# A new hand-written order table for a fused attention and feed-forward kernel, and one rule for its warm-up products

## The chip, the cores and the metric

The kernel runs on one core of a Trainium2 chip. The metric is device microseconds of one launch. Five engines work side by side: TensorE (PE; its weight loads are listed as PEld), VectorE (DVE), ScalarE (ACT), GpSimd (POOL) and SyncE (SP), which here only issues transfers. Each engine takes its instructions strictly in the order of its own list and waits at the head of that list, so an order of the lists is an order of the work.

## The reference: what is computed

The input x is one sequence of 2048 rows of 640 numbers. It is normalised by rows; the normalised rows feed two branches whose results are added to x.

```
xn  = layernorm(x)                              # 2048 x 640
q   = xn @ wq -> 32 heads of 20;  k = xn @ wk, v = xn @ wv   # one shared head of 20
p   = softmax(q k^T * 20**-0.5);  o = p v       # 32 heads x 2048 x 2048
A   = concat(o) @ wo
B   = relu(xn @ w1 + b1)**2 @ w2 + b2           # 640 -> 1536 -> 640
out = x + A + B
```

Almost all of the work outside TensorE is the exponential of 32 x 2048 x 2048 scores.

## The kernel before, in words

**Tiles.** A block is four heads by 512 query rows; there are 32 blocks, and each has 16 tiles of 128 keys. For one key tile the four heads make four score products of 128 x 512 into four banks of PSUM, called QK when ScalarE takes the exponential and DQK when VectorE does. Seven banks go round among the scores and the other products; the eighth collects the weighted sums of a block.

**Two ways to an exponential.** ScalarE takes two banks in one instruction (line 1328, names ACT0 to ACT695), 696 in all, and the product PV with v follows. The other way is a "set" (164 sets, one key tile of one block each): VectorE makes an integer approximation of the scores from each bank (line 1551, D1_n_i), three shifted copies of that table of 128 x 2048 are made by passes P1, P2 and P3, each either on GpSimd (line 1571, two joined ones line 2117) or on VectorE (line 1572), and the four terms are multiplied with v (DPV). Two of the four terms of a set (a = 0 and a = 3) can be added into another table instead of being multiplied: either by a transfer that GpSimd issues and that adds on landing (lines 1588, 2047, 2115; AD), or by VectorE (lines 1593, 2048). So of every set there are five choices.

**The opening.** The first rows of x come in four transfers of 128 rows (X0 to X3) and later ones in larger pieces (X4, X6, X8, and X12 for rows 1536 to 2047, line 753). Per 128 rows: statistics (lines 806 to 808, S and AG; VE is line 803 or 811), the power -1/2 on GpSimd (line 820, PW), the normalised rows (line 822, XN, on VectorE or GpSimd), a transpose on TensorE (lines 866 and 934, T) and its copy out of PSUM (lines 869, 871 and 937, TE). From these come kT (KTe, lines 885 and 949), the first queries (Q0 products, and their copies Qe0 on ScalarE, line 887) and v. A copy xb of x in device memory is made by SP (line 1152), and a transfer XA that GpSimd issues (line 1153) adds the bias b2 onto it; xb plus b2 is the residual that is added to the outputs much later (XR loads). SP waits for the copy TE2 before it issues wq (line 764) or xb. Before the first transposes TensorE makes products of constants (line 905, "warm-up products"), and later products of zeros onto the summing bank ("zero products", kT with zeros on line 729); in the planner's list both have the name fill, the second kind with the mark tail.

**The other work.** The feed-forward products FFN (960 products), their relu and square on VectorE (RL line 1054, SQ line 1062), the output products OUT and the last ones OF (line 729 for all of TensorE), the normalisation of blocks (TN line 1416, R on line 1422, CM on line 1452, with small transfers between) run between the scores.

**What sets the order.** A planner in the kernel first builds each engine's list by priorities. Then the table PLAN reorders it: for PE, DVE, POOL and SP each number says which of the instructions still left is next (0 is the first left, and n*k stands for n taken k times); "held" says for each POOL operation which VectorE operation it has to wait for, since some operations of the two (marked lock) are kept apart; and "on" has one digit for each choice: five digits a set, three for the passes (0 GpSimd, 1 VectorE) and two for the terms a = 0 and a = 3 (0 multiplied, 1 added by a transfer, 2 added by VectorE). ScalarE's list has no table and keeps its order. A function replay then walks through the reordered lists with a table of durations and gives out the PSUM banks and buffers; the waits follow from that. Behind replay a loop drops zero products that would fall where no block's sum is open.

## Time and profile before

| | |
|---|---|
| time, median of 3 runs | 665.14 us (664.26 to 666.17) |
| the profiled execution | 664.67 us |
| its span | 662.9 us |
| busy, ACT / PE / DVE / POOL | 649.2 / 655.0 / 627.0 / 533.1 us |
| first and last exponential on ScalarE | start at 12.17, end at 653.85 us |

The span runs from the first instruction to the last one in the profile; some 1.8 us of the execution lie around it. A row of a group reads: line, engine, operation, out<-in, shapes, count, then busy time and the mean of one in ns, then the idle time before them with what ended it. A row of the timeline has the start in us, the length in us, and the count of instructions merged into it. The starts of two neighbouring exponentials lie closer together than one lasts, so a stretch of n of them lasts n-1 spacings and one duration.

### The profile page before, as it was taken

What the parts mean: (1) busy time and instruction counts of PE and PEld (TensorE: products, weight loads), DVE (VectorE), ACT (ScalarE), POOL (GpSimd) and SP (SyncE); (2) the same over time, 40 slices, a digit from 0 to 9 for tenths busy, and PEclk for the clock granted to TensorE, in tenths of its full rate; (3) what the DMA queues carried; (4) which work ended last, traced back from release to release, by engine and by line L of the source; (5) the groups of instructions that cost most, each with busy time, mean ns of one, the idle gap of its engine ahead of it and who ended that gap; (6) DMA issues with size and microseconds to landing.
All of it is one profiled execution on the core that took longest, in us unless ns stands there. A gap on an engine that the chain in (4) does not pass through costs nothing. (4 is left out here: it accounts for less than half of the span.)

```text
span 662.9 us, 22377 instructions
## 1 busy us (share of the span) xinstructions
PE 655.0 (99%) x9569; PEld 212.6 (32%) x9570; DVE 627.0 (95%) x1125; ACT 649.2 (98%) x719; POOL 533.1 (80%) x528
## 2 busy tenths in 40 slices
PE   8999999999999999999999999999999999999997
PEld 4432222332322223333332222333233322223444
DVE  8979999999999999999999999999999999999997
ACT  7999999999999999999999999999999999999995
POOL 1629899898998889898999988888899989799300
PEclk9999999999999999999999999999999999999999
DMA  8694967788997995786956645798798655858731
GB/s 262 188 238 113 189 126 161 163 183 190 191 192 162 184 182 114 135 177 124 184 103 152 126 92 102 153 180 176 150 176 167 130 123 98 171 104 183 136 113 68
DMA packets 53528, 102.09 MB, mean 154 GB/s; under 512 B 15916, under 2 KB 31164, under 8 KB 53364
## 3 DMA queue, kind: packets, MB, share of 16 engines
q0 software_dynamic: 18544, 68.17, 55.7%
q1 hardware_dynamic: 34308, 32.11, 16.7%
q8 instruction: 75, 1.23, 0.8%
q10 hardware_dynamic: 576, 0.38, 0.2%
q14 instruction: 25, 0.20, 0.1%
HBM read 23.26 MB, written 10.01 MB: 50 GB/s over the span
## 5 line engine op out<-in xcount | busy, mean ns | idle before, releaser
L1328 ACT ACTIVATE PT<-ps 128x1024 bf16<-128x1024 f32 x696 | 640.1, 1125 | 1.8 <-PE ps L729 1.4
L1551 DVE TENSOR_SCALAR tx<-ps 128x512 uint16<-128x512 f32 x656 | 423.7, 682 | 20.8 <-PE ps L729 13.5
L1571 POOL INT64_ADD tx<-tx x369 | 391.2, 1130 | 56.7 <-PE ps L729 16.4
L729 PE MATMUL ps<-qT,kT 20*128 20x512 bf16 x2048 | 263.5, 385 | 0.3
L729 PEld LDWEIGHTS ps<-qT,kT 20*128 20x128 bf16 x2048 | 67.8, 91 | 253.1 <-ACT PT L1328 133.5
L729 PE MATMUL ps<-PT,vx 128*32 128x512 bf16 x1392 | 131.4, 384 | 0.0
L729 PE MATMUL ps<-tx,vxs 128*32 128x512 bf16 x1220 | 113.0, 384 | 0.6 <-DMA tx<-tx 0.5
L1588 POOL DMA_DIRECT2D tx<-tx x103 | 102.4, 994 | 7.7 <-POOL tx L1571 6.9
L729 PE MATMUL ps<-w_sb,big 128*32 128x320 bf16 x1536 | 82.7, 302 | 0.0
L729 PE MATMUL ps<-tx,vx 128*32 128x512 bf16 x864 | 81.3, 384 | 0.8 <-DMA tx<-tx 0.7
L729 PE MATMUL ps<-xnT,w_sb 128*32 128x512 bf16 x960 | 79.0, 383 | 0.0
L1572 DVE TENSOR_SCALAR tx<-tx 128x2048 uint16<-128x2048 uint16 x91 | 63.0, 705 | 0.5 <-DMA tx<-tx 0.3
L729 PEld LDWEIGHTS ps<-PT,vx 128*32 128x32 bf16 x1392 | 34.4, 95 | 39.5 <-issue 35.0
L729 PEld LDWEIGHTS ps<-w_sb,big 128*32 128x32 bf16 x1536 | 34.2, 96 | 30.9 <-issue 20.7
L729 PEld LDWEIGHTS ps<-tx,vxs 128*32 128x32 bf16 x1220 | 28.7, 95 | 36.6 <-issue 27.7
L1054 DVE TENSOR_SCALAR hT_tmp<-ps,b1col 128x512 bf16<-128x512 f32 x48 | 35.7, 743 | 1.5 <-PE ps L729 1.3
L729 PE MATMUL ps<-xnT,wq_sb 128*32 128x512 bf16 (+2 forms) x480 | 35.6, 356 | 0.0
L729 PE MATMUL ps<-wo_c,OC 128*32 128x320 bf16 x576 | 31.8, 301 | 0.0
L2117 POOL INT64_ADD tx<-tx x16 | 30.6, 1913 | 0.5
L729 PEld LDWEIGHTS ps<-tx,vx 128*32 128x32 bf16 x864 | 21.0, 95 | 27.1 <-issue 20.5
L729 PEld LDWEIGHTS ps<-xnT,w_sb 128*32 128x32 bf16 x960 | 19.4, 95 | 25.7 <-issue 17.4
L1416 DVE COPY OR<-ps 128x512 f32<-128x512 f32 x30 | 20.4, 681 | 0.9 <-PE ps L729 0.6
(91 smaller groups left out, 242.3 us busy)
## 6 DMA issues: line engine op xcount, KB each, us to landing
tx<-tx POOLq DMA_DIRECT2D x111, 512.0 KB, 5.8
tx<-tx POOLq DMA_DIRECT2D x7, 1024.0 KB, 9.3
w_sb<-in_B_w_dram SPq DMA_DIRECT2D x8, 480.0 KB, 9.3
big<-OR SPq DMA_DIRECT2D x71, 40.0 KB
xb<-in_A_x_dram SPq DMA_DIRECT2D x1, 2560.0 KB, 12.7
xb<-b2r POOLq DMA_DIRECT2D x1, 2560.0 KB, 19.1
xr<-xb SPq DMA_DIRECT2D x16, 160.0 KB, 3.5
out_dram<-out_sb SPq DMA_DIRECT2D x15, 160.0 KB, 3.3
```

What stands on the lines that cost most here:

```text
L729: return lambda e: e.matmul(out_(), l, val(r), start=val(start), stop=val(stop), tile_position=tp, skip_group_check=loose)
L1054: o = Op(f"RL{qc}_{f}", "DVE", 0.66, [lambda e: e.tensor_scalar(out=hT_tmp[:, k % 2, :], in0=ps[:, at(bk), :], scalar1=b1col[:, f:f + 1], ...
L1328: o = Op(f"ACT{st_['j']}", "ACT", ACB + ACM * n, [lambda e: e.activation(out=PT[:, slots[0].n:slots[0].n + n, :], in_=src(), func=AF.Exp, ...
L1416: tn = op(f"TN{b}", "DVE", 0.60, lambda e: e.tensor_copy(out=OR[:, a, :], in_=ps[:, PVB, :]), [lastpv] + or_users[a], prio=0)
L1551: d1 = op(f"D1_{n}_{i}", "DVE", 0.60, lambda e: e.tensor_scalar(out=L()[:, cs].bitcast(U16), in0=ps[:, ref.n, :], scalar1=XA, scalar2=XB, ...
L1571: fns = dict(POOL=lambda e, T=T, j=j: e.int64_add(out=T().bitcast(I64), in0=L().bitcast(I64), in1=TSTEP * j * 0x0001000100010001), DVE=lam ...
L1572: DVE=lambda e, T=T, j=j: e.tensor_scalar(out=T().bitcast(U16), in0=L().bitcast(U16), scalar1=TSTEP * j, scalar2=None, op0=ALU.add))
L1588: p = op(f"AD{a}_{n}", "POOL", ADDUR, lambda e, src=src, dst=dst: e.dma_start(dst(), src(), accum_op=ALU.add), dp + [ad_last.get(k)], dma= ...
L2117: fn = lambda e, x=x: e.int64_add(out=two(*sorted((x["ref"][2].n, x["ref"][3].n))).bitcast(I64), in0=two(*sorted((x["ref"][0].n, x["ref"][ ...
```

## The change

Every list of PLAN is new. Most entries of the choices stay: 54 of the 820 digits of "on" differ. Counted over the sets, passes on GpSimd go from 401 to 395 and on VectorE from 91 to 97; terms that are multiplied go from 193 to 191, those added by a transfer from 125 to 127, and those added by VectorE stay 10.

Read against the planner's lists, which are the same in both kernels, the new order table says this, among much else:

- SP: `X8, X12, b2, wq, xb, w11, b1, w10` becomes `X8, b2, xb, X12, wq, b1, w10`; some weights (w11, w12, w13, w20 to w23) come later among the small transfers.
- PE: `K0, Q0_0, Q0_1, Q0_3, K1, Q0_2, K2, V0_0, V0_1, K3, QK0, QK1` becomes `K0, Q0_1, Q0_0, Q0_3, Q0_2, K1, V0_1, K2, QK1, QK0`, with K3 behind.
- Warm-up products: ahead of the first transpose 15 become 12, between it and the first weighted sum 3 become 5, and one stands behind that sum. Of the zero products 12 stay in the kernel before and 8 in the new one.
- POOL: `PW13, PW12, XA, PW14` becomes `PW12, XA, PW13, PW14`; the XA issue comes behind the statistics of tile 12 in both.
- DVE: ahead of XN12 and XN13 there were `AG12, VE13, S14a, VE12, S15b, KTe5, Ve2`; between VE12 and XN12 there are now `TE10, TE11, S13b, S14a, S14b, AG13, KTe5, VE13, S15b, Ve2`.
- DVE, up to set 144: ten passes more than before; behind it fewer, so that six more remain.
- PE changes between score products and other products 1322 times instead of 1318. Behind the last score product QK695 there were 9 OUT, 40 OF, 3 PV and 1 DPV; now there are 8, 40, 3 and 3.

The second part is in the loop behind replay: a warm-up product that would come after the first weighted sum has begun is left out.

```diff
     "PE": (
-        "0*39 1 2 16 21 4 0 28 1*2 2 0 15 1*2 2*3 4 2 21 2*3 30 4 3 2 30 0 1 0 7 0 5 4 0*4 1 0*3 49 0*2 1*7 0*2 1 2 1 0 7 1*7 0*3 1*3 3 2*2 1 0 1*7 2 3 2 0 2 3 2 0*2 1*11 2 5 2*2 "
...
+        "0*8 55 39 0 68 0*2 2 4 0 42 3*6 4 3*2 4 3 5 3 6 5 17 6 3 29 3 0 2 4 55 3 9 3*2 5*2 27 44 5*2 2 5*3 7 5*2 0 4 3 1 5 4 12 3 1 2 0 6*2 1*10 2 0 8 0 1*3 0*4 1*2 36 1 8 2*7 1 "
...
     "DVE": (
...
     "POOL": (
-        "0*15 2 0*7 1 0 2 5 0*2 4 0 5 3 5 6*2 5 7 9 5 2 0 5 12 3 7 5 3 0 4 0*2 1 4 1 4 0 1 0 4 0 4 1*2 0*2 3 0 1 2 3 0*2 4 2 4 0*2 1 2 0*2 1 0 1 0 2 0*2 1 3*2 0*2 2 0 2*5 1 2 3 "
...
+        "0*2 1 0*22 2 1*2 5 3 6 7 4 7 0 7 2 4 6 8 5 14 0 3*2 0*3 3 8 2 3 1 2 1 0 1 0 1 4 0*3 2 5 0*3 1 2 3 0 3 6 2 1 0 2 0 1 0*2 4 1 0*2 2*2 0 4 0 1 0 3 0 3*2 4 3*2 6 0 1 4 0 1 6 "
...
     "SP": (
-        "0*10 2 1 0 5 2 0*2 2*3 4 1*2 2 5*3 12 2 10 18 9 1*2 19 2 10 17 6 0 15 7 5 2 16 11 4 10 20 8 4 0 14 7 13 3 20 3 7 6 12 9 5 16 19 4 9*2 3 5 20 11 0 10 11 8 10 8 10 4 14 12 "
...
+        "0*6 1 2 0*2 1 0 7 5 6*2 8 12 6 11 7 1 0 8 5 14*2 13 0 2*2 1 8 1 7 18 4 17*2 8*2 15*2 17 2 11 5*2 18*2 12 10 5 1 13 12*2 5 4 20 0 5 8 10 4 12 14 12 0 14*2 11 8 7 16 9 3 2 "
...
     "held": (
-        "-*2 31*2 51 - 57 51 57 30 - 57 30 - 51 - 51 - 102 - 102 103 -*2 132 126 -*6 146*2 149 -*2 174*2 149 -*17 174 216 186 - 224*2 - 224 - 224 - 241 224 -*6 252 241 -*2 252 260 "
...
+        "-*2 29 30 50 51 57*2 51 57*2 - 57*2 50 -*6 106 -*3 130 141 - 147*5 121 - 141 -*7 179*2 -*7 192 - 173 192 - 212 - 212 - 212 223 212 -*4 242 -*2 241 242 - 252 242 -*3 252 "
...
     "on": (
-        "01000000000000100000100110000000010000100000001001000100001000000000000000001010000100000000110011100001000010000200001000010001100001010000001100011000010010100011010010"
-        "00010000100011100000100100001001010000100010001010000100011000010010110101000010000110001000010100100001000100000000001001010001100000001010000011101000111000000001000110"
-        "01111000200000000010110000001000011000011101001000000100010100002000010100100000000000001000110000000001000000000100011000000000000000000010000100100000011000000000000010"
-        "10010001100101000110100100001001011000000001001010110111001000000100100101000010000101010000010000101001001010001100101000000010100111000000000100001000010010100000000010"
-        "00000010100000000000000100001001010000101000001010100100001100000000000001010010000000001001000100100011001011001101110211122111201112211120"),
+        "01000000000000100000010110000000010000100000001001000100011000000000000010001010000100000000010110100001000010001200001000010001101001000000001100011000010010100011010110"
+        "00010000100011100000100100001001010000100010000010100100011000010010110001010010001110001000010100100001000100001001001001010001100000001010000011101000111000000001000110"
+        "00111000200000000010100000001000011000011011001000000100010100002000010100110000001000001000011000001001000000000100011000000001000000000010000101000000011000000000000010"
+        "00010010100001000110100100001001011000000001001010100111001001000010100001000010001101010000010000101101011010010100011000000010100111000000000100001000010010100000000010"
+        "10001000100000000000000100011001010000100010000010100100001100000000000001010010000000001001000100100011000011001101110211122111201112211120"),
@@ -2145,11 +2149,12 @@
             es_.sort(key=lambda o: o.start)
             for o in es_:
                 o.ends[0], o.ends[1] = o is es_[0], o is es_[-1]
-        open_, kept = set(), []
+        open_, kept, begun = set(), [], False
         for o in order_all:
             if o.sums is not None:
                 (open_.discard if o.ends[1] else open_.add)(0)
-            if o.name == "fill" and o.tail and not open_:
+                begun = True
+            if o.name == "fill" and (not open_ if o.tail else begun):
                 continue
             kept.append(o)
         order_all[:] = kept
```

## The prediction

> **What bounds the kernel now.** I read the share of each engine first, then the row of the exponentials, then the timeline of ScalarE alone.

> ```profile
> PE 655.0 (99%) x9569; PEld 212.6 (32%) x9570; DVE 627.0 (95%) x1125; ACT 649.2 (98%) x719; POOL 533.1 (80%) x528
> ...
> L1328 ACT ACTIVATE PT<-ps 128x1024 bf16<-128x1024 f32 x696 | 640.1, 1125 | 1.8 <-PE ps L729 1.4
> ```

> ```profile
> 12.17 152.22 ACT L1328 ACTIVATE PT<-ps 128x1024 bf16<-128x1024 f32 x165 [0.23 <-PE ps L729]
> 164.71 127.69 ACT L1328 ACTIVATE PT<-ps 128x1024 bf16<-128x1024 f32 x139 [0.32 <-PE ps L729]
> 292.65 170.95 ACT L1328 ACTIVATE PT<-ps 128x1024 bf16<-128x1024 f32 x186 [0.25 <-PE ps L729]
> ...
> 556.13 97.72 ACT L1328 ACTIVATE PT<-ps 128x1024 bf16<-128x1024 f32 x106 [0.19 <-PE ps L729]
> ...
> 657.06 1.63 ACT L1662 ACTIVATE out_sb<-ps 128x320 bf16<-128x320 f32 x4 [3.21 <-PE ps L729]
> ```

> ScalarE makes one exponential after the other from 12.17 to 653.85 us (556.13 + 97.72), with 1.8 us of idle time before all 696. So the execution is a head of 12.2 us, 641.7 us of exponentials, and a tail of 9.0 us, in which ScalarE waits 3.21 us for TensorE. The change touches neither the number nor the shape of the exponentials. Only three things can move the time: the head, the spacing of the exponentials, and the tail. The spacing is (164.71 - 12.17) / 165 = 0.9245 us in the first stretch, (292.65 - 164.71) / 139 = 0.9204 us in the second. A short stretch shows what it is when little is late:

> ```profile
> 560.88 11.11 ACT L1328 ACTIVATE PT<-ps 128x1024 bf16<-128x1024 f32 x12
> ```

> Here it is (11.11 - 1.125) / 11 = 0.908 us. All 695 spacings at that value would give 695 x (0.9219 - 0.908) = 9.7 us; 0.9219 is the mean, (641.7 - 1.0) / 695. That is the whole room in the middle, spread over many small waits for a bank that TensorE filled late. The chain of work that ended last shows one kind of lateness, a sum by transfer behind a run of passes on GpSimd:

> ```profile
> 454.88 8.08 DMA tx<-tx
> 462.95 0.04 issue
> 463.00 49.98 PE ps L729 x737
> ```

> **The head.** Here the new order is to be followed link by link.

> ```profile
> 10.35 0.45 PE L729 MATMUL ps<-xnT,wq_sb 128*20 128x128 bf16 x20
> 10.62 0.45 PE L729 MATMUL ps<-xnT,wk_c 128*20 128x128 bf16 x20
> 11.01 0.41 PE L890 MATMUL ps<-wv_c,xnT 128*128 128x20 bf16 x10
> 11.35 0.46 PE L729 MATMUL ps<-xnT,wk_c 128*20 128x128 bf16 x20
> 11.74 0.40 PE L729 MATMUL ps<-qT,kT 20*128 20x512 bf16 x4
> ```

> ```profile
> 10.85 0.28 ACT L887 ACTIVATE qT<-ps 128x128 bf16<-128x128 f32 x1 [0.28 <-PE ps L729]
> 11.02 0.82 ACT L802 ACTIVATE OC<-tx,mv 128x640 bf16<-128x640 bf16 x1
> 11.74 0.19 ACT L802 ACTIVATION_READ_ACCUMULATOR OC<-tx,mv 128x1 f32 x1
> ```

> The first scores start at 11.74 behind K3 (11.35), though the last query copy ended at 11.13. With K3 behind the scores, and Q0_2 ahead of K1 (one product group earlier, 10.62 - 10.35 = 0.27 us), the scores can start at about 11.3. ScalarE's list is unchanged, so the statistics at 11.02 still stand ahead of the first exponential; they move up with the query copy by 0.2 to 0.3 and end at about 11.7 instead of 11.93. So the first exponential comes 0.2 to 0.4 us earlier; I take -0.3. The last K tile is then late instead, but the second pair of score steps is its first reader, some 2 us on.

> **XA against VectorE.**

> ```profile
> 28.53 1.81 POOL L1153 DMA_DIRECT2D xb<-b2r  x1
> ```

> ```profile
> 6.98 1.50 DVE L822 TENSOR_SCALAR big<-tx,mv,rstd 128x640 bf16<-128x640 bf16 x4
> ...
> 28.86 0.24 DVE L969 CAST vx<-ps 128x80 bf16<-128x80 f32 x1
> 29.02 1.46 DVE L822 TENSOR_SCALAR big<-tx,mv,rstd 128x640 bf16<-128x640 bf16 x2
> ```

> Four normalisations took 1.50 us at 6.98; two took 1.46 at 29.02, under the issue of XA. At 1.50 / 4 the two cost 0.75 us, so the issue cost VectorE about 0.7. The copy out of PSUM at 28.86 ran in 0.24 us under the same issue, so not everything is held. The new order puts ten VectorE operations, some 3 us, between VE12, for which GpSimd waits before XA, and XN12: the normalisations then miss the issue. Whether the copies TE and the statistics in their place are held, no row shows; the ends are nothing (as for the copy) and 0.7. I take nothing, since the copies read PSUM like the one shown. The excess of the first stretch, 165 x (0.9245 - 0.9204) = 0.7 us, is all that ScalarE can show of the opening; I give 0.5 of it to this move and the better spaced transposes. [...]

> **X12 behind xb.** SP now waits for TE2 (the end of the second ScalarE copy, about 10 us) ahead of X12, and X12's 640 KB stand behind xb's 2560 KB.

> ```profile
> 10.66 1.39 SPq L1152 DMA_DIRECT2D xb<-in_A_x_dram  x1
> ```

> ```profile
> xb<-in_A_x_dram SPq DMA_DIRECT2D x1, 2560.0 KB, 12.7
> ```

> ```profile
> 23.98 0.48 DVE L806 BATCH_NORM_STATS2 OR<-tx 128x6 f32<-128x320 bf16 x1
> ...
> 25.06 0.48 DVE L949 TENSOR_SCALAR kT<-ps,nk 128x256 bf16<-128x256 f32 x1
> ```

> xb took 12.7 us to land with wq ahead of it. At worst X12 lands a quarter of that after xb: 10.0 + 12.7 + 3.2 = 25.9; if half of the 12.7 was waiting for wq, at 10.0 + 6.4 + 3.2 = 19.6. Its first reader is the statistics of tile 12 at 23.98. In between the cover is 4.4 us, and at the worst end VectorE stands for 1.9 us with KTe4 (25.06) queued behind it, and TensorE and ScalarE behind that. I take no cost, since wq's bytes are no longer ahead; the end stays for a rival.

> **The passes.**

> ```profile
> L1571 POOL INT64_ADD tx<-tx x369 | 391.2, 1130 | 56.7 <-PE ps L729 16.4
> ...
> L1588 POOL DMA_DIRECT2D tx<-tx x103 | 102.4, 994 | 7.7 <-POOL tx L1571 6.9
> ...
> L1572 DVE TENSOR_SCALAR tx<-tx 128x2048 uint16<-128x2048 uint16 x91 | 63.0, 705 | 0.5 <-DMA tx<-tx 0.3
> ```

> ```profile
> 80.00:120.00 40.00, 40.00 (x542) 11.30 (x538) 38.89 (x66) 40.00 (x44) 37.17 (x36) 1.00 0.72 150
> ...
> 560.00:600.00 40.00, 39.90 (x509) 10.69 (x501) 39.03 (x68) 39.95 (x44) 35.26 (x34) 1.00 0.73 142
> ```

> GpSimd loses six passes at 391.2 / 369 = 1.06 us and gets two issues at 0.99: -4.4 us. VectorE gets six passes at 63.0 / 91 = 0.69: +4.2 us. Two windows show VectorE idle for 1.1 and 1.0 us in 40, GpSimd for 2.8 and 4.7. So the relief of GpSimd is worth between nothing and 4.4, the load of VectorE between nothing and 4.2; both are hidden as long as the other engines' waits end with ScalarE. I take nothing for both: the two ends are nearly equal and of opposite sign. The same goes for the redrawn order of everything else. Lost cover for VectorE would be its 1 us in 40.

> **The tail and the small things.**

> ```profile
> 20.05 0.60 PE L729 MATMUL ps<-PT,vx 128*32 128x512 bf16 x8
> ```

> Two weighted-sum products take 0.60 us, the last one drains for 384 ns, so one costs 0.22. Behind QK695 two more of them and one output product less stand on TensorE: 2 x 0.22 less 0.14 (an output product has 320 columns against 512, 0.22 x 320 / 512) = +0.3, in the tail, where ScalarE already waits for TensorE: it counts in full. The four extra changes of score and other products and the two products saved in total (-0.44) lie under ScalarE elsewhere and cost nothing. The dropped warm-up product is one of 0.22 us; what it covered is idle TensorE time.

> **The sum.** 664.67 (this execution) - 0.3 - 0.5 + 0.3 = 664.2. The median of the runs is 0.47 above this execution; on its scale 664.6 us, 0.1% below 665.14.

> **The rivals.**

> *GpSimd's relief shows.* Three of ScalarE's gaps end with TensorE waiting for a sum by transfer, two of them here:

> ```profile
> 163.91 0.10 PEld L729 LDWEIGHTS ps<-tx,vx 128*32 128x32 bf16 x4 [0.72 <-DMA tx<-tx]
> ```

> ```profile
> 291.67 0.10 PEld L729 LDWEIGHTS ps<-tx,vxs 128*32 128x32 bf16 x4 [0.83 <-DMA tx<-tx]
> ```

> With the list 4.4 us shorter such sums are issued earlier. Against it speaks that the two new sums need landing time too. Between 1.6 (these two) and 4.4 us: 3.0 in the middle, 661.6 us.

> *VectorE becomes the bound* (the other side). Ten of its added passes come before set 144, 6.9 us of load where about 1 us in 40 is idle. Where two fall into one 40 us window, 1.4 us meets 1.0 and scores for the approximation are freed late, so TensorE stands and ScalarE with it. From there on each further pass costs its 0.7. For it: 38.89 and 39.03 busy of 40. Against it: in the first of these windows ScalarE is busy for all of the 40.00 us all the same. Six passes shown in full: 664.6 + 4.2 = 668.8 us.

> *X12 is late.* 1.9 us at VectorE, no gain from the opening: 664.6 + 0.5 + 1.9 = 667.0 us. The change then does not do what it says, since the opening gets longer.

> *The clock drops.* Three warm-up products fewer stand ahead of the transposes.

> ```profile
> 4.50:7.50 3.00, 2.73 (x12) 0.79 (x11) 2.90 (x11) 2.41 (x8) 0.00 (x0) 1.00 0.92 269
> ```

> ```profile
> 2.57 2.64 PE L905 MATMUL ps<-hT_tmp,OR 128*128 128x512 bf16 x7
> 5.48 2.08 PE L905 MATMUL ps<-hT_tmp,OR 128*128 128x512 bf16 x8 [0.27 <-DVE OR L806]
> 7.47 1.54 PE L866 MATMUL ps<-ident,big 128*128 128x128 bf16 x20
> ```

> The first seven took 2.64 us, the next eight 2.08 with waits in them; early products are slower. If the transposes ran at the early rate they would take about 1.5 us more: 666.1 us. The granted clock is 1.00 in the window, and fewer products leave gaps below 1 us. [...]

> **How the numbers follow.** Forecast 0.37; GpSimd 0.29; VectorE 0.22; X12 0.08; clock 0.04. About 0.3% (2.0 us) is what a measurement of this kernel can tell from no change. Faster takes GpSimd (0.29) and 0.04 of the forecast's spread; slower takes VectorE, 0.05 of X12 and 0.03 of the forecast; the rest, 0.37, is the same. The forecast's own range is 662.4 to 666.7, half of the two engines' ends, 2.2 down and 2.1 up. The range for all reaches from 659.9 (GpSimd's whole 4.4, and 0.3 more if head and opening reach their ends of 0.4 and 0.7) to 669.3 (VectorE's case without the opening's 0.5).

> **What would show it.** Right: the first exponential at 11.8 to 12.0; two normalisations of tiles 12 and 13 in 0.8 to 0.9 us; the first stretch's spacing near 0.920; 9.0 to 9.4 us from the last exponential to the end. Wrong: statistics of tile 12 that wait for a transfer; VectorE idle below 0.7 us in 40 with more time of TensorE ended by it; a spacing in the middle off 0.9204 by more than 0.003, which is 2 us.

## The result, and the profile after

The new kernel takes 671.43 us (median of 7, 669.22 to 683.05), the kernel before 664.81 in the same comparison. The ratio is 1.0094, with a 95% interval of 1.0075 to 1.0112: slower by 0.9%, some 6 us, and outside the range that the prediction gave. The ratios here leave out executions more than 1.5% above the fastest of their kernel (here those of 681.09 and 683.05 us); the medians and ranges of times leave out none. The profiled execution of the new kernel is the one of 671.43 us, its span 669.6. Its lines lie 4 lower in the code: the exponentials, line 1328 before, are line 1332 here.

The shares and the row of the exponentials, from the page of the new kernel:

```profile
PE 656.9 (98%) x9543; PEld 212.3 (32%) x9545; DVE 632.5 (94%) x1131; ACT 651.0 (97%) x719; POOL 529.3 (79%) x520
...
PE 69%; DMA 10%; DVE 8%; POOL 7%; ACT 3%; issue 2%; SPq 0%; DVEq 0%; POOLq 0%
...
L1332 ACT ACTIVATE PT<-ps 128x1024 bf16<-128x1024 f32 x696 | 642.0, 1114 | 7.2 <-PE ps L733 6.6
```

The same row of the chain in the kernel before:

```profile
PE 26%; POOL 3%; DMA 2%; DVE 0%; issue 0%; POOLq 0%
```

ScalarE now stands 7.2 us before its exponentials instead of 1.8. In the chain that ended last, transfers, VectorE and GpSimd have 25% together, where they had 5%. All of that comes in steps, as the timeline of ScalarE shows (start, length, exponentials merged into the row, and the idle time before it):

```profile
11.72 8.43 ACT L1332 ACTIVATE PT<-ps 128x1024 bf16<-128x1024 f32 x9
20.38 10.19 ACT L1332 ACTIVATE PT<-ps 128x1024 bf16<-128x1024 f32 x11 [0.23 <-PE ps L733]
31.05 2.85 ACT L1332 ACTIVATE PT<-ps 128x1024 bf16<-128x1024 f32 x3 [0.49 <-PE ps L733]
34.24 9.72 ACT L1332 ACTIVATE PT<-ps 128x1024 bf16<-128x1024 f32 x10 [0.34 <-PE ps L733]
44.45 69.07 ACT L1332 ACTIVATE PT<-ps 128x1024 bf16<-128x1024 f32 x75 [0.49 <-PE ps L733]
114.65 97.27 ACT L1332 ACTIVATE PT<-ps 128x1024 bf16<-128x1024 f32 x106 [1.14 <-PE ps L733]
212.40 31.54 ACT L1332 ACTIVATE PT<-ps 128x1024 bf16<-128x1024 f32 x34 [0.48 <-PE ps L733]
245.09 6.61 ACT L1332 ACTIVATE PT<-ps 128x1024 bf16<-128x1024 f32 x7 [1.15 <-PE ps L733]
...
332.82 86.61 ACT L1332 ACTIVATE PT<-ps 128x1024 bf16<-128x1024 f32 x94 [0.28 <-PE ps L733]
419.75 11.18 ACT L1332 ACTIVATE PT<-ps 128x1024 bf16<-128x1024 f32 x12 [0.33 <-PE ps L733]
431.22 12.98 ACT L1332 ACTIVATE PT<-ps 128x1024 bf16<-128x1024 f32 x14 [0.29 <-PE ps L733]
...
636.84 23.94 ACT L1332 ACTIVATE PT<-ps 128x1024 bf16<-128x1024 f32 x26 [0.55 <-PE ps L733]
664.43 1.66 ACT L1666 ACTIVATE out_sb<-ps 128x320 bf16<-128x320 f32 x4 [3.64 <-PE ps L733]
```

The counts give the number of an exponential: 9 + 11 + 3 + 10 + 75 = 108, so the row at 114.65 begins with exponential 108. Set against the start of the exponential with the same number in the trace of before:

| exponential | before | after | later by |
|---|---|---|---|
| 0 | 12.17 | 11.72 | -0.45 |
| 20 | 30.65 | 31.05 | 0.40 |
| 40 | 49.56 | 51.00 | 1.44 |
| 107 | 110.91 | 112.33 | 1.42 |
| 108 | 111.88 | 114.65 | 2.78 |
| 247 | 239.76 | 242.91 | 3.15 |
| 248 | 240.66 | 245.09 | 4.43 |
| 341 | 326.45 | 331.31 | 4.86 |
| 448 | 424.67 | 431.22 | 6.55 |
| 695 | 652.55 | 659.58 | 7.03 |

So the head gained 0.45 us, the opening up to exponential 40 lost 1.89, seven single exponentials in the middle lost the other 5.6 (1.36 at 108, 0.74 at 214, 1.28 at 248, 0.54 at 342, 0.46 at 436, 0.44 at 448 and 0.82 at 670), and between them small losses and gains cancel: from exponential 40 to 107 the distance stays at 1.4. (The expectations below list six of these, without the one at 214, and give them 5.6 together; the six make 4.9.) The tail is 0.2 us shorter (669.6 - 636.84 - 23.94 = 8.8 us, before 9.0).

Behind two of the steps in the middle stands a sum by transfer. At exponential 108 the timeline of GpSimd and of TensorE says:

```profile
102.98 0.87 POOL L1592 DMA_DIRECT2D tx<-tx  x1 [0.30 <-POOL tx L1575]
...
111.57 4.08 POOL L1575 INT64_ADD tx<-tx  x4 [1.61 <-DMA tx<-tx]
...
113.67 0.40 PE L733 MATMUL ps<-tx,vxs 128*32 128x512 bf16 x4 [1.38 <-POOL tx L1575]
```

GpSimd waits 1.61 us until the sum issued at 102.98 has landed, because the next pass (P2 of set 17) writes into a buffer that this sum still reads. Behind that pass stands P3 of set 16, and TensorE waits 1.38 us for that one. At exponential 248:

```profile
224.71 0.86 POOL L1592 DMA_DIRECT2D tx<-tx  x1
...
232.87 1.25 POOL L1575 INT64_ADD tx<-tx  x1 [1.70 <-DMA tx<-tx]
234.06 1.21 POOL L2119 DMA_DIRECT2D tx<-tx  x1
...
243.87 0.40 PE L733 MATMUL ps<-tx,vx 128*32 128x512 bf16 x4 [1.19 <-DMA tx<-tx]
```

Here P3 of set 49 waits 1.70 us for the sum of 224.71, the joined sum of set 50 behind it is issued that much later, and TensorE waits for its landing. (In both places the weight load ahead of the waiting product shows 1.68 us of idle time; the expectations below name that number.)

In the opening TensorE stands for a bank, and VectorE for the transposes of tiles 12 and 13 that come behind:

```profile
30.62 0.39 PE L733 MATMUL ps<-qT,kT 20*128 20x512 bf16 x2 [0.52 <-ACT PT L1332]
...
32.21 0.89 DVE L941 COPY xnT<-ps 128x640 bf16<-128x640 bf16 x2 [1.68 <-PE ps L938]
```

### The profile page after: what moved, and what is told of

It is laid out like the page before. It is cut to its first block, busy times and chain, and to the rows that moved or that the text cites. A ratio compares the mean times of both kernels' runs of the same rounds, so it can differ in the third digit from the quotient of the medians.

```text
span 669.6 us, 22323 instructions
## 1 busy us (share of the span) xinstructions
PE 656.9 (98%) x9543; PEld 212.3 (32%) x9545; DVE 632.5 (94%) x1131; ACT 651.0 (97%) x719; POOL 529.3 (79%) x520
## 4 chain that ended last, share of the span: by engine, by line
PE 69%; DMA 10%; DVE 8%; POOL 7%; ACT 3%; issue 2%; SPq 0%; DVEq 0%; POOLq 0%
PE ps L733 69%; DMA tx<-tx 10%; POOL tx L1575 6%; DVE tx L1555 4%; ACT PT L1332 3%; DVE tx L1576 1%; DVE big L1066 1%; DMA tx<-in_A_x_dram 1%; DVE hT_tmp L1058 1%; POOL tx L1592 0%; DVE OR L1420 0%; DVE OC L1456 0%; PE ps L938 0%; POOL tx L2121 0%; PE ps L870 0%
## 5 line engine op out<-in xcount | busy, mean ns | idle before, releaser
L1555 DVE TENSOR_SCALAR tx<-ps 128x512 uint16<-128x512 f32 x656 | 423.0, 682 | 19.5 <-PE ps L733 12.7
L1592 POOL DMA_DIRECT2D tx<-tx x102 | 100.3, 988 | 11.2 <-POOL tx L1575 7.4
L1576 DVE TENSOR_SCALAR tx<-tx 128x2048 uint16<-128x2048 uint16 x97 | 69.6, 731 | 2.5 <-DMA tx<-tx 2.3
## 6 DMA issues: line engine op xcount, KB each, us to landing
xb<-in_A_x_dram SPq DMA_DIRECT2D x1, 2560.0 KB, 10.8
xb<-b2r POOLq DMA_DIRECT2D x1, 2560.0 KB, 18.0
```

The costliest lines, as they stand in the source:

```text
L1555: d1 = op(f"D1_{n}_{i}", "DVE", 0.60, lambda e: e.tensor_scalar(out=L()[:, cs].bitcast(U16), in0=ps[:, ref.n, :], scalar1=XA, scalar2=XB, ...
L1576: DVE=lambda e, T=T, j=j: e.tensor_scalar(out=T().bitcast(U16), in0=L().bitcast(U16), scalar1=TSTEP * j, scalar2=None, op0=ALU.add))
L1592: p = op(f"AD{a}_{n}", "POOL", ADDUR, lambda e, src=src, dst=dst: e.dma_start(dst(), src(), accum_op=ALU.add), dp + [ad_last.get(k)], dma= ...
```

## The experiments

Edits of the order table are shown in the names of the lists, since the numbers of PLAN can't be read. Each time stands beside runs of the kernel before on the same chip (664.5 to 665.0 us, medians).

**The opening against the rest.** Everything that the new table starts before 45 us, by the times that replay gives, was put back into the old order, and the other way round.

```diff
 e1: new kernel, all lists
-first 45 us in the new order
+first 45 us in the old order
 e2: kernel before, all lists
-first 45 us in the old order
+first 45 us in the new order, with the new rule for warm-up products
```

> The new kernel with the opening of the kernel before: everything that the old table starts in the first 45 us (154 to 173 instructions of TensorE, 54 of ScalarE, 133 of VectorE, 23 of GpSimd) in the old order, the rest in the new order. Theory A: the loss has two separate sources, the opening (ScalarE's exponential number 40 came 1.4 us later than before, although the first one came 0.45 us earlier) and single stands in the middle (exponentials 108, 248, 342, 436, 448, 670: 5.6 us together) that belong to the new order there. Then this kernel takes 671.4 - 1.4 = about 670.0 us, and its trace still shows the stands at exponentials 108 and 248 (1.1 us each). Theory B: the stands in the middle follow from the opening, which leaves GpSimd behind; then this kernel is back at about 665.5 us and the stands are gone.

> The kernel before with the opening of the new one: what the new table starts in the first 45 us in the new order, the rest in the old order, and the new rule for warm-up products. Theory A (two separate sources): 664.8 + 1.4 = 666.2 us, the first exponential 0.45 us earlier, exponential 40 about 1.4 us later than before, and no further growth behind it. Theory B (the middle follows from the opening): about 671 us, with stands near exponentials 108 and 248.

e1 took 673.05 us (667.22 to 681.57), ratio 1.0101 (1.0052 to 1.0150). Its stand at exponential 108 did not go but grew, and something came behind it. The row of TensorE, then the windows (busy time of PE, PEld, DVE, ACT, POOL, and after them the granted clock):

```profile
113.34 0.62 PE L744 MATMUL ps<-tx,vxs 128*32 128x512 bf16 x4 [2.28 <-POOL tx L1586]
```

```profile
110.00:115.00 5.00, 2.72 (x31) 0.61 (x31) 2.27 (x5) 2.31 (x4) 3.77 (x4) 0.75 0.35 66
115.00:120.00 5.00, 5.00 (x41) 0.89 (x37) 3.00 (x5) 3.52 (x4) 2.27 (x3) 0.50 0.67 138
...
135.00:140.00 5.00, 5.00 (x48) 1.21 (x45) 3.54 (x6) 3.06 (x3) 1.97 (x3) 0.52 0.56 107
140.00:150.00 10.00, 10.00 (x144) 3.01 (x142) 9.63 (x18) 9.78 (x12) 8.36 (x9) 1.00 0.51 108
```

Behind a stand of 2.28 us TensorE ran at half its clock for 27 us, though it was busy all the time, and ScalarE fell to 3.1 to 3.5 us of work in 5: exponential 108 was 3.09 us late, exponential 124 13.67. The one execution of e1 at a clock of 1.00 took 667.22 us; the others had 0.979 to 0.995. So theory A held for the stand, which belongs to the new order in the middle and not to the opening; its time of 670.0 us was met neither by the median nor by that one execution, and no theory had the clock.

e2 took 668.32 us, ratio 1.0053 (1.0034 to 1.0073). Exponential 40 came 1.29 us late, 1.92 after the first one's gain of 0.63, as theory A had it. But the distance grew on to 2.5 us at exponential 165 and 4.0 at 230, and fell back to 3.0 at the end: the old order, pushed late by the opening, gets stands of its own. Theory A is right on the opening; that nothing follows from it is wrong.

**XA ahead of the power for tile 13.**

```diff
 kernel before, GpSimd
-PW13  PW12  XA    PW14
+PW12  XA    PW13  PW14
```

> The kernel before with one exchange on GpSimd: the issue of XA (1.81 us) ahead of the power for tile 13 instead of behind it. Theory C: this exchange is what costs the opening its time. The power for tile 13 then comes 1.8 us later, the normalisation of tile 13 with it, and VectorE, which has the copy of the transposes queued behind it, stands; about 1.4 to 2 us at exponential 33, 666.2 to 666.8 us in all. Rival: VectorE's order around the transposes costs it, and not the issue; then this kernel stays within 0.5 us of 664.8.

666.1 us, ratio 1.0027 (1.0010 to 1.0045); exponential 30 came 1.48 us late. Theory C holds for the old order, and VectorE's timeline shows how:

```profile
29.03 0.86 DVE L835 TENSOR_SCALAR big<-tx,mv,rstd 128x640 bf16<-128x640 bf16 x1
31.01 0.45 DVE L835 TENSOR_SCALAR big<-tx,mv,rstd 128x640 bf16<-128x640 bf16 x1 [1.12 <-POOL rstd L833]
```

VectorE stands 1.12 us for the power of tile 13. But the new kernel has no such wait: there VectorE's list has other work at that place. So the price of theory C is right in the old order and says nothing of the new one; the opening is settled by the bank experiment below.

**The head alone.**

```diff
 kernel before, TensorE and the query copies on ScalarE
-K0 Q0_0 Q0_1 Q0_3 K1 Q0_2 K2 V0_0 V0_1 K3 QK0 QK1
+K0 Q0_1 Q0_0 Q0_3 Q0_2 K1 V0_1 K2 QK1 QK0 V0_0 K3
```

> The kernel before with the new order of TensorE at the first scores alone (queries of head 2 ahead of the second K tile, QK1 and QK0 ahead of K3) and the exchange of the first two query copies on ScalarE. If the 0.45 us that the first exponential gained come from these links, as the prediction had it, the first exponential starts at 11.7 to 11.9 us here too, and the kernel takes 664.4 us, or a little more where K3 is then late for the second pair of scores. If they come from the shorter row of warm-up products, the first exponential stays at 12.1 to 12.2 us.

665.84 us, ratio 1.0011 (0.9997 to 1.0025). The first transposes and the first exponential:

```profile
7.80 1.54 PE L879 MATMUL ps<-ident,big 128*128 128x128 bf16 x20 [0.18 <-DVE big L835]
...
12.12 1.02 ACT L1341 ACTIVATE PT<-ps 128x1024 bf16<-128x1024 f32 x1
```

The first rows of x landed later in this execution, so the start of the first exponential says nothing; from the first transpose to it are 4.32 us, against 12.17 - 7.47 = 4.70 before. The links bring 0.38 us, as predicted. But exponential 5 came 0.54 us late, and the gain is lost. With K3 behind the scores and nothing else changed, VectorE waits 0.54 us for K3's product (until 12.72) before it can copy it, the next statistics and the normalisation behind them come later, and TensorE stands 0.82 us for it, until 15.58. In the new kernel the copy of K3 stands behind the statistics in VectorE's list and waits for nothing.

**Loads beside a sum.**

```diff
 e5: new kernel, SP
-w20 at 101 us, wo0 at 104 us
+w20 at 60 us, wo0 at 82 us
 e9: kernel before, SP
-SL2 OM2_1 BC0_0 QD7_0 SM3 wo0
+wo0 SL2 OM2_1 BC0_0 QD7_0 SM3
```

> The new kernel with two weight loads of 480 KB issued earlier on SP: w20 at about 60 us instead of 101, wo0 at about 82 instead of 104. In the new kernel the sum issued at 102.98 us landed after 8.51 us, while these two loads were under way, and GpSimd stood 1.6 us for it with a pass behind, for which TensorE then stood 1.68 us. Theory D (the loads make the sum late): the sum lands in 5.5 to 6.5 us, the stand at exponential 108 goes, 1.4 us less, 670.0 us, and the granted clock stays at 1.00. Theory E (sums of this density land late anyway, and the new order leaves too little room behind them): the sum still takes 8 us or more and the stand stays.

> The kernel before with one weight load, wo0 (480 KB), issued on SP some 6 us earlier than there, at about 101 us, 1 us ahead of the sum that GpSimd issues at 102.5; all else in the old order. In the kernel before that sum landed after 5.49 us. Theory D (a load beside a sum makes it late): it lands after 8 to 9.5 us, as in the new kernel (8.51) and in the new kernel with the old opening (9.41). Where the old order has room behind the sum, TensorE does not stand and the time stays at 664.8; where it has not, it stands 1 to 2 us and the time is about 666. Rival (the order of the sums makes them late): it lands after 5.5 to 6.5 us.

e5 took 668.53 us, ratio 1.0056 (1.0041 to 1.0071), some 2.5 us less than the new kernel, or 1.5 if only executions with a mean clock of 0.999 or more are compared (668.49 against 670.04), near the 1.4 of theory D. Its profiled execution ran at a mean clock of 0.66 from end to end and took 827.91 us, so its trace says nothing of the stands. The trace of e9 shows what a load does to a sum. The issues of the load and of the sum, with the KB and the time to landing,

```profile
wo_c<-in_A_wo_dram SPq DMA_DIRECT2D x1, 480.0 KB, 3.7
```

```profile
tx<-tx POOLq DMA_DIRECT2D x1, 512.0 KB, 7.1
```

against the new kernel, and the kernel before, in which no load was under way at the issue:

```profile
tx<-tx POOLq DMA_DIRECT2D x1, 512.0 KB, 8.5
wo_c<-in_A_wo_dram SPq DMA_DIRECT2D x1, 480.0 KB, 8.9
```

```profile
tx<-tx POOLq DMA_DIRECT2D x1, 512.0 KB, 5.5
```

A load issued 2.4 us ahead of the sum made it 1.6 us later; less than theory D expected (8 us and more), but this load landed 1.3 us after the sum was issued, and the one in the new kernel 9.6 us after it. In e9 TensorE did not stand and the time stayed (664.68 us, ratio 1.000, 0.999 to 1.001): the old order has room behind this sum, the new one has not.

**A pass that waits, and what stands behind it.**

```diff
 e6: new kernel, GpSimd
-P2_17  P3_16  P2_18
+P3_16  P2_17  P2_18
-P3_49  AD_50 (joined)  P1_51
+AD_50 (joined)  P1_51  P3_49
```

> The new kernel with two passes moved on GpSimd's list. P3 of set 16 goes ahead of P2 of set 17, which waits for a sum's landing; P3 of set 49, which waits for the sum of set 48, goes behind the joined sum of set 50 and the next pass. Theory E (a pass that waits for a sum holds up what is queued behind it, and the new order has such passes close behind their sums): both stands of TensorE, 1.68 us each at 111.9 and 242.2 us, shrink to under 0.7 us, exponential 108 loses about 1 us less and exponential 248 about 1.5 us less, 668.9 us in all. Theory D (late landing alone): the stand at 108 stays at 1 us or more, since the pass behind P2 of set 17 is needed nearly as early.

669.76 us, ratio 1.0070 (1.0043 to 1.0098). At exponential 248 theory E was right: the stand is gone (later by 3.13 at 244 and 3.17 at 248). At 108 theory D was: the stand split into two smaller ones, and exponential 120 was 2.92 us late, 1.7 more than exponential 107, against 1.3 more in the new kernel. The pass that was moved back is needed nearly as early; there only a sum that lands in time helps.

> The new kernel with the two weight loads early and the two passes moved, and its own opening. If the sources are separate, this is 666.4 us (the same with the old opening) plus the 1.9 us of the opening, 668.3 us; exponential 40 comes 1.3 us later than before, no stand follows at exponentials 108 and 248, and the small stands at exponentials 342, 436 and 670 (0.5 to 0.8 us each) stay only if they do not follow from the opening.

Both edits together (e5 and e6): 668.47 us, ratio 1.0061 (1.0046 to 1.0076). The sum at 103.37 landed in 5.7 us, and exponentials 108 and 248 lost nothing (1.77 and 1.96 late, against 1.81 at 107). So with the loads away the sum is in time and the stand at 108 gone, which e5's trace could not show. The total is no better than e5's within the intervals; one stand stayed:

```profile
317.10 1.20 POOL L2062 DMA_DIRECT2D tx<-tx  x1
...
326.02 2.05 POOL L1586 INT64_ADD tx<-tx  x2 [2.36 <-DVE tx L1566]
...
330.02 0.40 PE L744 MATMUL ps<-tx,vx 128*32 128x512 bf16 x4 [1.30 <-POOL tx L1586]
```

The sum of 317.10 landed at 325.86 (8.76 us, no load beside it, but another sum issued 1.6 us ahead), 0.2 us before GpSimd went on. The row names VectorE; in e6, where the same pass waited 2.00 us, it names the transfer.

```diff
 e12: as e10, GpSimd
-P2_75  P1_77  AD0_76  P1_75  P2_76
+P1_77  AD0_76  P1_75  P2_75  P2_76
```

> The kernel of the mended middle with one more pass moved on GpSimd: P2 of set 75, which waits for the first sum of set 74 (landing after 8.76 us there, issued 1.6 us behind another sum), goes behind P1 of set 75, for which TensorE stands 1.30 us at 328.7. Theory E (a pass that waits for a sum holds up what is queued behind it): the stand shrinks to under 0.5 us, exponential 342 loses at most 0.3 us instead of 1.15, and the kernel takes 667.5 us, 1.0 less than with the mended middle. Rival: the stand comes from VectorE, whose tables GpSimd waits for in the same row; then it stays above 1 us.

667.30 us, ratio 1.0039 (1.0026 to 1.0051). TensorE's waits between 300 and 345 us are gone, and ScalarE runs from 227.80 to 439.2 us without a gap:

```profile
227.80 211.41 ACT L1343 ACTIVATE PT<-ps 128x1024 bf16<-128x1024 f32 x230 [0.26 <-PE ps L744]
```

The sum landed in 7.39 us in this execution, 1.4 us faster, so the trace alone could not tell the order from luck; that all 6 executions (666.41 to 667.77) lie at or below the 4 of e10 (667.77 to 669.64) speaks for the order.

**Old opening and mended middle.** e1 with the edits of e5 and e6.

> The new kernel with the opening of the kernel before up to 45 us, the two weight loads early, and the two passes moved. If the opening and the stands near exponentials 108 and 248 are separate sources, the three add up: 671.4 - 1.9 - 1.4 - 1.6 = 666.5 us, and the stands behind exponential 260 remain (about 2 us). If new stands take their place, it stays above 668 us.

666.39 us, ratio 1.0027 (1.0013 to 1.0041): the time that was expected, though not in every part, for ScalarE still lost 1.1 us at exponential 248 (TensorE waits 0.97 us for VectorE there), and the later stands did not come. The sum at 101.89 landed in 6.4 us here, against 9.4 in e1, which has the same opening and the load of wo0 issued 0.6 us ahead of it; in e1 w20 is early already, so one load is enough.

**A stand, and the clock behind it.**

```diff
 kernel before, at six places (q a score pair, x a sum by transfer)
+k = next(i for i, o in enumerate(seq["PE"]) if o.name == q)
+late = next(o for o in seq["PE"][k + 1:] if o.on)
+late.deps.append(next(o for o in seq["POOL"] if o.name == x and o.on))
```

> The kernel before with six added waits: at six places between 155 and 620 us one instruction of TensorE waits for the landing of a sum that it does not read, so that TensorE stands there for about 1, 1.5 or 2 to 3.5 us. In the new kernel with the old opening a stand of 2.28 us was followed by 27 us at a granted clock of 0.50, and stands of 1.68 us in the new kernel by none. Theory F (the length of a stand decides): behind the stands under 1.7 us the clock stays at 1.00, behind those over 2.2 us it falls to 0.50 for some 25 us, and the kernel takes 675 to 700 us. Rival: that fall was a disturbance from outside; then the clock stays at 1.00 throughout and the time is 664.8 us plus what ScalarE stands, 6 to 9 us.

684.4 us, ratio 1.0289 (1.0249 to 1.0328). The six stands in TensorE's timeline, and the windows behind the third and the last:

```profile
160.34 0.37 PE L729 MATMUL ps<-qT,kT 20*128 20x512 bf16 x1 [1.52 <-DMA tx<-tx]
246.30 0.61 PE L729 MATMUL ps<-xnT,w_sb 128*32 128x512 bf16 x8 [1.20 <-DMA tx<-tx]
328.93 0.37 PE L729 MATMUL ps<-qT,kT 20*128 20x512 bf16 x1 [1.61 <-DMA tx<-tx]
425.54 0.42 PE L729 MATMUL ps<-xnT,w_sb 128*32 128x512 bf16 x4 [2.13 <-DMA tx<-tx]
509.95 0.37 PE L729 MATMUL ps<-qT,kT 20*128 20x512 bf16 x1 [1.09 <-DMA tx<-tx]
591.99 0.37 PE L729 MATMUL ps<-qT,kT 20*128 20x512 bf16 x1 [2.93 <-DMA tx<-tx]
```

```profile
330.00:334.00 4.00, 4.00 (x38) 0.77 (x34) 2.99 (x6) 2.45 (x3) 3.01 (x3) 0.57 0.48 97
334.00:340.00 6.00, 6.00 (x105) 2.22 (x105) 5.29 (x9) 5.95 (x7) 4.84 (x6) 1.00 0.78 151
...
596.00:600.00 4.00, 4.00 (x34) 0.79 (x34) 2.88 (x5) 2.65 (x3) 0.16 (x1) 0.50 0.90 160
```

The stands of 1.09, 1.20 and 1.52 us left the clock at 1.00. Behind those of 1.61, 2.13 and 2.93 the trace's clock record has 3.4, 3.4 and 10.2 us at 0.50. Theory F holds in the main, with a shorter fall than the 25 us expected and a limit below its 1.7 us, since the stand of 1.61 us is among those that cost the clock. The new kernel's own stand at exponential 108, 1.38 us in the profiled execution, is a little shorter; in three of its seven executions the mean clock was below 1.00 (0.992, 0.982, 0.972, with 675 to 683 us). That a longer stand there cost them the clock is likely, but they have no trace.

**The first 20 us of the new order.**

```diff
 kernel before, all lists
-first 20 us in the old order
+first 20 us in the new order
```

> The kernel before with the first 20 us of the new order and the old order behind, XA behind the power for tile 13 as before. If the new opening up to there only brings the 0.38 us between the first transpose and the first exponential, and the loss begins with XA, the first exponential starts 4.3 us after the first transpose instead of 4.7, the gain is kept, and the kernel takes 664.4 us, the fastest of all. If the later K3 takes it back, as where the head's links were taken alone, it takes 665 to 665.8 us.

665.19 us, ratio 1.0003 (0.9994 to 1.0013). The first exponential starts 11.77 - 7.50 = 4.27 us after the first transpose, and exponential 150 is still 0.16 us early; then single gaps of 0.2 to 0.8 us come, and no gain can be measured.

**The banks in the opening.** A score pair takes two neighbouring banks, and replay hands them out as they come free. In the list that it gives for the new kernel QK20 has banks 4 and 5, QK22 has 0 and 1, and QK19 behind them finds single banks only.

```diff
 new kernel, TensorE
-QK17  QK18
+QK18  QK17
```

> The new kernel with one exchange on TensorE: the score pair QK18 ahead of QK17 instead of behind it. A score pair takes two neighbouring banks. By the list of banks that replay gives out, the new kernel leaves no two neighbours free for QK19: QK20 has taken banks 4 and 5, QK22 0 and 1, and QK19 has to wait until exponential 20 frees bank 4 beside 3. TensorE stands 0.52 us there on the chip (until 30.62 us), ScalarE 0.49 behind it, the transposes of tiles 12 and 13 come behind QK19, and VectorE stands 1.68 us for them. With the exchange QK19 gets banks 5 and 6 at once. Theory G (the banks cost the opening): the stand at 30.1 us goes, the gap of ScalarE at 31.05 too, exponential 40 comes 1.5 to 1.9 us earlier than in the new kernel, 669.6 us in all. Theory C (XA ahead of the power for tile 13): nothing of XA is changed, so exponential 40 stays 1.4 us later than before.

ScalarE's gaps at 31.05, 34.24 and 44.45 us are gone:

```profile
20.44 39.90 ACT L1343 ACTIVATE PT<-ps 128x1024 bf16<-128x1024 f32 x43 [0.23 <-PE ps L744]
```

Exponential 40 starts at 49.23, 0.33 us earlier than in the kernel before and 1.77 earlier than in the new one. Theory G is right and theory C, for this kernel, wrong: one exchange of two score pairs brings back the whole opening, with XA where it was. The time is 672.04 us all the same, ratio 1.0083 (1.0052 to 1.0113): the stand at exponential 108 has become 1.84 us long, and behind it the clock is at 0.50 for 10.2 us. The executions at a clock of 1.00 took 665.85 to 667.74 us.

> The new kernel with everything that the runs point to: the exchange of QK17 and QK18, the two weight loads early, and the three passes moved on GpSimd. If the opening and the three stands are separate sources, 667.3 us (the same without the exchange) less 1.9, about 665.4 us, level with the kernel before; if the head's gain of 0.4 us is kept whole, 664.4 to 665.

With the exchange, the loads and the three passes together: 665.73 us, ratio 1.0007 (0.9992 to 1.0022), level with the kernel before. ScalarE's longest stretch and its row on the page:

```profile
23.41 304.47 ACT L1343 ACTIVATE PT<-ps 128x1024 bf16<-128x1024 f32 x331 [0.21 <-PE ps L744]
```

```profile
L1343 ACT ACTIVATE PT<-ps 128x1024 bf16<-128x1024 f32 x696 | 640.3, 1124 | 3.0 <-PE ps L744 2.4
```

At exponential 341 it is 0.6 us ahead of the kernel before, 1.1 behind at the end: two stands of TensorE are left, 0.69 us for a pass at 327 and 1.16 for a sum at 413. None of the versions beats the kernel before.

## Why the prediction was wrong

**The step that failed** is the sentence "The same goes for the redrawn order of everything else": it was taken as nothing, beside two engines whose loads cancel. In the profiled execution it cost 5.6 us behind exponential 40, and the clock there was at 1.00. Two ways of that are shown: loads of 480 KB moved beside a sum (in e1 one is enough: the sum lands in 9.4 us, against 6.4 in e7), and a pass that waits for a sum's landing put ahead of a pass or an issue that TensorE needs. The kernel before has such waits too, but short ones: its longest idle time of a weight load that ends with a sum is 0.83 us, against 1.68 in the new kernel. In three of the seven executions the mean clock was lower as well (0.992, 0.982 and 0.972). Of the 5.6 us behind exponential 40, 1.8 are left in e10 and 0.3 in e12, by lists alone, and e14, with the exchange, is level with before. Why sums land late more often in the new order, where no load is beside them, stays open.

**The opening** was given -0.5 us and lost 1.9. The part that was worked out came true: XN12 and XN13 miss XA and take 0.43 and 0.40 us, 0.83 where 0.8 to 0.9 was predicted. But the -0.5 did not come of it: with the banks mended (e13), ScalarE takes 37.45 us from the first exponential to exponential 40, before 37.39, and in the new kernel 39.28. What failed is that only the moves named in the change were costed. The order of the score pairs, counted there among much else, left QK19 without two neighbouring banks, and e13 shows that this alone is the loss. The prediction, and the description of the kernel ahead of it, also say that ScalarE's list is unchanged. That is false: PLAN has a short row for ScalarE too, which exchanges Qe0_0 with Qe0_1, and exponentials 5 with 6, 19 with 20 and 21 with 22. e13 keeps that row and recovers the opening, so the row is not the cause; but the pairs that it names are the ones that wait for banks, and it should have been read.

**The head**, -0.3: the size is right, though the first exponential at 11.72 lies just outside the 11.8 to 12.0 that was named: 0.39 from the first transpose (11.72 - 7.41 = 4.31 against 4.70), and e4 has the same 0.38 from the predicted links alone. That the late K3 costs nothing is right in the new kernel (exponential 5 still 0.45 early) and wrong where the rest of the order does not follow it. Its first reader is also not the second pair of scores but its copy on VectorE, as e4 shows.

**The tail**, +0.3: wrong in sign and small. ScalarE's wait grew from 3.21 to 3.64 us, but the tail is 0.2 us shorter in all.

**X12 behind xb**: taken as nothing, and right. No operation of VectorE between 20 and 45 us waits for a transfer; X12 landed at 23.16, inside the bounds, and its first reader starts at 23.86. This rival is out.

**VectorE becomes the bound**: its 668.8 us is nearer to the result than the forecast, but its mechanism is not what happened. The loss comes in single stands that end with a sum or a bank, and e14 has all of the new passes and is level with before. One sign of it did come, for VectorE is idle for 0.36 us in the second window of 40, below the 0.7 that was named:

```profile
560.00:600.00 40.00, 39.99 (x520) 10.99 (x512) 39.64 (x69) 39.87 (x44) 34.41 (x33) 1.00 0.69 134
```

But ScalarE loses 0.08 us there (39.87 against 39.95), and in e14 VectorE is as busy in it (39.57) and ScalarE for all of the 40.00.

**GpSimd's relief** went the other way. GpSimd has less to do, and its passes wait for transfers, by the view of its waits (total us, times, longest), before and after:

```profile
POOL tx L1571 <- DMA tx<-tx: 0.5, 1, 0.5
```

```profile
POOL tx L1575 <- DMA tx<-tx: 8.2, 9, 1.7
```

**The clock** was a rival with the right engine and the wrong place: not the transposes (they took 1.54 us as before, and the granted clock is 1.00 from the start of its record at 4.43 us), but, in some executions, a stand in the middle. Its price does not follow from its rows either: at 2.64 / 7 = 0.38 us a product against 0.22, transposes of 1.54 us would take about 1.1 us more, not 1.5. Its small chance was the author's estimate; the gaps below 1 us that speak against it are shorter than every stand here that cost the clock (1.61 us and more).

The sign that was named for a wrong prediction did come: from exponential 40 to 695 the spacing is (659.58 - 51.00) / 655 = 0.929 us, before (652.55 - 49.56) / 655 = 0.921.

## What to carry to other kernels

An order drawn from a table of durations is worth the room that it leaves behind events that vary: ask of each transfer what is the next instruction in the queue that waits for it, and what stands behind that one. The waits that a reordering removes can be read from the old profile, the waits that it makes cannot; where every list is redrawn, a cost of nothing for "the rest" has a long side upwards and none downwards. And where two neighbouring buffers are taken at once, an exchange of two equal steps can cost as much as a wrong engine.

## What the runs showed of the hardware

**TensorE's clock fell to half behind stands of 1.61 us and more.** Over all traces but e5's stands of up to 1.52 us left the granted clock at 1.00, and 1.61, 1.84, 2.13, 2.28 and 2.93 us brought it to 0.50, for 3.4, 10.2, 3.4, 27.3 and 10.2 us, with TensorE busy throughout. That cost 4.3 us behind the stand of 1.84 us (in e13 exponential 108 was 1.51 us late, exponential 120 5.83) and 10.6 behind that of 2.28 us (e1).

**A sum by transfer (512 KB) lands in 5.9 us at the median in the new kernel and in 5.8 in the one before; a few late ones decide.** Over 7 us took 31 of 111 sums in the new kernel and 11 of 111 before. Among sums issued while no other was in flight, over all traces but e5's, only those with a load of 480 KB beside them took more than 8 us (8.51, 8.83, 8.97 and 9.41; 7.1 in e9), and none without a load more than 7.6. Of those issued with two or more others in flight, 9 of 13 in the new kernel and 3 of 12 before took over 7 us. That the crowd of sums makes them late is not tested here.

**XA's issue slowed a normalisation on VectorE and did not stop it.** In e3 one normalisation took 0.86 us under the issue (from 29.03, the issue from 28.53 to 30.35) and so ended 0.46 us ahead of its end; in the new kernel, away from the issue, one took 0.43.
